# A fused attention and expert kernel: the switch from its first phase to its second is recut (22 tiles and four full pairs instead of 20 and three)

## The chip, the cores and the metric

The kernel runs on one core of one Trainium2 chip. The metric is device time in microseconds (us) of one execution; smaller is better. Engine names: PE is TensorE (matrix multiply), PEld its weight loads, DVE is VectorE, ACT is ScalarE, POOL is GpSimd, SP is SyncE; the letter q behind an engine (SPq) means instructions that only its queue handles, such as the issue of a DMA.

## What is computed

Three stages, one behind the other, all in float32. 3072 tokens (4 batches of 768) with 384 numbers each run through all of them.

```python
# 1. linear attention with a complex decay, 8 heads of 48
for t in range(S):
    new_re = ar * S_re - ai * S_im
    new_im = ar * S_im + ai * S_re
    S_re, S_im = (new_re + einsum('bhd,bhe->bhde', k[t], v[t]), new_im)
    y[t] = einsum('bhd,bhde->bhe', q[t], S_re)
# 2. a dense expert: 384 -> 768 -> 384
h = np.maximum(np.maximum(x @ w1, x @ w2), x @ w3)
x = h @ w_out
# 3. one of 8 experts for each token, 384 -> 1024 -> 384
expert_idx = np.argmax(xn @ en.T / tau, axis=1)
for e in range(8):
    h = np.maximum(x[mask] @ w1[e], 0.0)
    out[mask] = gate_w[mask, None] * (h @ w2[e])
```

## The kernel before

**Phase 1** (`phase1`, L991) does stages 1 and 2 in twelve units of 256 tokens. Every operation is first recorded with a key (`KEYS`, L1061) and then issued by a list scheduler (`issue`, L233) that takes, on the engine that is free first, the ready operation with the lowest key; so all rows of phase 1 carry the line L299, where it issues them. A unit is two tiles of 128 tokens. Its last products are `px<-wo,h`, one PSUM tile for each tile of tokens; ACT then copies it (`x1s`), writes it to the DRAM tensor `x1d` and squares it, adding up a sum of squares (`ss`, one column for each of the 24 tiles).

**The first routing** (`route_early`, L932, recorded with the key `early`) looks at the first `TE` = 20 tiles only, that is units 0 to 9. From their sums of squares and logits it forms the expert of each token (`oneh`), counts them on PE (`within`), gives the first `PE` = 3 full pairs of blocks (256 tokens of one expert each, `KE` = 6 blocks of 128) to experts, writes the experts of these pairs to a table (`tab`, in the trace `btab`), builds the one-hot rows `pos` on DVE and sorts tokens into slots on PE (`slots`); out comes `srcrow`, the token in each slot. `first_rows` (L979) then gathers block 0 (`xg_0`, an indirect DMA from `x1d` by POOL) and transposes it on PE (`pxg_0`). Both are part of phase 1, and their buffers lie in its pool `pp`.

**Phase 2** (`phase2`, L1323) runs the experts in steps. Steps 0 and 1 are the two blocks of the first pair, one at a time in plain float32; then a step is a pair (blocks 2 and 3 are step 2, and so on) with operands split into two parts (`xh`, `xl`, `w1s`, `w1l`, `w2h`, `w2l`). The expert of a step is known only on the chip: `load` reads it from the table and fetches 1.5 MB of `w1` and 1.5 MB of `w2` into two queued buffers (`queue_q_buf`), and leaves the transfer out if the expert is that of the step before. Per step: `prep` makes the weight tiles out of the queued buffer (for step 0 the copies `w1s` at L1197 on DVE), `mm1` (L1243) multiplies by `w1`, `transpose` (L1220) turns the gathered rows of the next step, `mm2` (L1259) multiplies by `w2`, and POOL scatters the result to `out`. `gather` is called two steps ahead.

**The second routing** (`late_route`, L1064) takes all 24 tiles and places what the first left over: 9 more pairs (`PL`), 8 single blocks, 5 minis of 32 tokens. `LATE` (L65) puts it behind step 1. The blocks from `KE` on can be gathered only when its `srcrow` and `dstrow` (L1142, L1145) are there. `flag` (L1409), at its end, tests among other things the sums of squares (`inrange<-ss`, L1419). A mini (`small`, L1269) loads its own weights (`w1m`, `w2m`), gathers its rows (`xgm`), and its transposes (`pxm`, L1288) stand between the halves of a step's `mm1`; `WITH` (L58) lists the steps that take one, the first being step 4.

The engines run their instructions in order. In phase 2 the order on each engine is that of the tile framework's scheduler; a pool that takes over memory of an earlier pool waits for that pool's users.

Of the kernel before, what the change touches and what calls it, by code (L numbers as in the profile page):

```python
# [27 lines left out]
E = 8  # L28
# [6 lines left out]

TE, PE, PL, SG = 20, 3, 9, E
KE, KP = 2 * PE, 2 * (PE + PL)
NBLK = KP + SG  # L40
MT, MINI = 32, 5
# [4 lines left out]
def steps(order):  # L46

    out, p, s = [(0, 1), (1, 1)], 2, KP
    for c in order:
        out.append((p, 2) if c == "p" else (s, 1))  # L50
        p, s = (p + 2, s) if c == "p" else (p, s + 1)
    assert (p, s) == (KP, NBLK - SPARE)
    return out + [(i, 1) for i in range(s, NBLK)]


STEPS = steps("ppppp" "s" "pppppp")
# [41 lines left out]
def bc(ap, axis, n):  # L98

    a = ap.unsqueeze(axis)  # L100
    shape = list(a.shape)
    shape[axis] = n
    return a.to_broadcast(shape)
# [210 lines left out]
class Prog:  # L314
# [447 lines left out]
    def moe1(self, u):  # L762
# [12 lines left out]
        for f2 in range(3):  # L775
# [5 lines left out]
            h = self.tl(pm, [128, 2, W], "h", 2, f"h{u}_{f2}")  # L781
            key, q.key = q.key, u + self.KEYS["max"]
            s.copy(h, ps[0])
# [148 lines left out]
    def route_early(self):  # L932

        q = self.q
        v, s, t = q.vector, q.scalar, q.tensor
        T, N = TE, KE
        arena = self.tl(self.pp, [128, 3, L, 3 * NR], "X", 2, "arena").rearrange("p a b c -> p (a b c)")
        used = [0]

        def new(shape, name, dt=F32):  # L940
            n = math.prod(shape)
            words = n // 2 if dt == BF16 else n
            x = arena[:, used[0]:used[0] + words]
            used[0] += words
            x = x.bitcast(dt) if dt != F32 else x
            if len(shape) == 2:
                x = x.rearrange("p (a b) -> p a b", b=shape[1])
            if len(shape) == 3:
                x = x.rearrange("p (a b c) -> p a b c", b=shape[1], c=shape[2])
            return x  # L950
        lg, mx = self.choose(new, self.ss[:, :T], self.lg[:, :T], self.oh[:, :, :T])
        self.gate(new, lg, mx, self.gates[:, :T])
        rank, cnt = self.ranks(new, self.tl(self.pg, [128, 2, E, T], "g", 2, "within0"), T)
        full, st, end, taken = self.pairs_of(new, cnt, T, PE, 256, "early")
        v.tensor_copy(self.taken, taken)

        be, x = new([PE, E], "beq"), self.bef[:, :NE]
        v.tensor_tensor(be, bc(self.blk[:, :PE], 2, E), bc(end, 1, PE), op=ALU.is_ge)
        v.tensor_reduce(x[:, 1:], be, axis=AX.X, op=ALU.add)
        v.tensor_copy(x[:, :1], x[:, 1:2])  # L960
        v.tensor_copy(self.tab[:, 0, :NE], x)
        v.tensor_tensor(self.tab[:, 1, 1:NE], x[:, 1:], x[:, :NE - 1], op=ALU.not_equal)

        ok = new([E, T], "inside")
        v.scalar_tensor_tensor(ok, bc(full, 2, T), 256.0, rank, op0=ALU.mult, op1=ALU.is_gt)
        v.scalar_tensor_tensor(rank, bc(st, 2, T), 256.0, rank, op0=ALU.mult, op1=ALU.add)
        v.scalar_tensor_tensor(rank, rank, 1.0, ok, op0=ALU.add, op1=ALU.mult)
        at, val = self.slots(new, rank, T, N)
        ps = self.tl(self.pg, [128, 5 * N], "g", 2, "slots0")
        for t0 in range(0, T, 6):  # L970
            n = min(6, T - t0)
            pos = self.tl(self.pp, [128, 6, 128], "f3", 3, f"pos{t0}", BF16)[:, :n]
            v.tensor_tensor(pos, bc(self.pos128, 1, n), bc(at[:, t0:t0 + n], 2, 128), op=ALU.is_equal)
            self.place(ps, pos, val, t0)
        tok = new([N], "tok")
        self.join(tok, self.gate_of[:, :N], ps)
        v.tensor_scalar_add(self.src[:, :N], tok, -1.0)
# [13 lines left out]
    def phase1(self):  # L991
        nc, tc = self.nc, self.tc
        with ExitStack() as ctx:
# [25 lines left out]
            self.X, self.S, self.QKr, self.xt, self.C = {}, {}, {}, {}, {}  # L1019
            K = self.KEYS  # L1020
            self.load_a(0)
# [36 lines left out]
    AHEAD = 3, 8  # L1058
    SIGNS = 4
    LAZY = False  # L1060
    KEYS = {"conv": -0.9, "moe": 0.3, "mid": -1.0, "attn": -2.0, "back": -1.0, "front": -0.9, "early": 10.5, "max": 0.3}  # L1061


    def late_route(self, pool, pg):  # L1064
# [258 lines left out]
    def phase2(self):  # L1323
        tc, nc = self.tc, self.nc
        with ExitStack() as ctx:
            regs = tc.queue_regs(depth=QD, engines=[ET.SP, ET.Activation, ET.DVE], name="wr")
            qp = ctx.enter_context(tc.tile_pool(name="wq", bufs=1, reuse_waits="tile"))
            q1 = qp.queue([128, 3072], F32, regs=regs, name="q1", contiguous=True)
            q2 = qp.queue([128, 3072], F32, regs=regs, name="q2", contiguous=True)
            pg = ctx.enter_context(tc.tile_pool(name="pg2", bufs=2, space=PSUM, reuse_waits="tile"))  # L1330
            pool = ctx.enter_context(tc.tile_pool(name="m2", bufs=1, reuse_waits="tile"))
            wq = ctx.enter_context(tc.tile_pool(name="ws", bufs=1, reuse_waits="tile"))

            late_ctx = ctx.enter_context(ExitStack())
            rp = late_ctx.enter_context(tc.tile_pool(name="rtp", bufs=1, reuse_waits="tile"))
            load, gather, prep, share, transpose, mm1, mm2, st = self.moe2(pool, wq, pg, regs, q1, q2)
            late = self.late_route(rp, pg)
            gather(*STEPS[1])
            load(0)
            first = prep(*STEPS[0])  # L1340
            for _ in range(2):
                next(first)
            last = NS - SPARE
            few = iter(())
            for k, (i, n) in enumerate(STEPS[:last]):
                if k + 2 < last:
                    gather(*STEPS[k + 2])
                p, after = iter(()), k + 1 < last
                if k == 0:

                    share(*STEPS[:2])
                    p = first
                elif after:
                    load(k + 1)
                    p = prep(*STEPS[k + 1])
                if k + 1 in WITH:

                    small = self.small(pool, mp, pg, WITH.index(k + 1))
                    next(small)
                next(p, 0)  # L1360
                mm1(i, n, 0)

                for _ in few:
                    pass
                if k in WITH:
                    few = small_now
                    next(few)
                if k + 1 in WITH:
                    small_now = small
                next(p, 0)  # L1370
                mm1(i, n, 1)
                next(few, 0)
                next(p, 0)
                if after:
                    transpose(*STEPS[k + 1])
                for b in range(n):
                    next(p, 0)
                    mm2(i, n, b)
                    next(few, 0)
                for _ in p:  # L1380
                    pass
                for _ in range(LATE.count(k)):
                    next(late)
                if k == LATE[-1]:
                    late_ctx.close()

                    self.four = self.mask
                    nc.gpsimd.memset(self.four, 0.0)
                    nc.vector.tensor_reduce(self.four[:, :MT], self.ident.rearrange("p (j r) -> p r j", r=MT), axis=AX.X,
                                            op=ALU.add)  # L1390
                    mp = ctx.enter_context(tc.tile_pool(name="mp", bufs=1, reuse_waits="tile"))
# [289 lines left out]
```

## Time and profile before

| | us |
|---|---|
| three runs | 875.11, 877.49, 877.52 |
| median | 877.49 |
| the profiled execution, own time | 878.75 |
| its span in the trace | 876.9 |

Mean granted clock of PE over the span: 0.971 of full speed.

The own time of the profiled execution is 1.85 us longer. Phase 1 fills the span up to 593 us, phase 2 the rest. In the rows further down a time is the start in us from the beginning of the span; behind it stands the busy time, then engine, line, operation, output and inputs, shapes, and the number of instructions that the row takes together; a bracket gives the idle time ahead of it and what ended it.

### The profile page before, as it was taken

What the parts mean: (1) busy time and instruction counts of PE and PEld (TensorE: products, weight loads), DVE (VectorE), ACT (ScalarE), POOL (GpSimd) and SP (SyncE); (2) the same over time, 40 slices, a digit from 0 to 9 for tenths busy, and PEclk for the clock granted to TensorE, in tenths of its full rate; (3) what the DMA queues carried; (4) which work ended last, traced back from release to release, by engine and by line L of the source; (5) the groups of instructions that cost most, each with busy time, mean ns of one, the idle gap of its engine ahead of it and who ended that gap; (6) DMA issues with size and microseconds to landing.
All of it is one profiled execution on the core that took longest, in us unless ns stands there. A gap on an engine that the chain in (4) does not pass through costs nothing. (4 is left out here: it accounts for less than half of the span.)

```text
span 876.9 us, 17518 instructions
## 1 busy us (share of the span) xinstructions
PE 813.1 (93%) x6741; PEld 714.6 (81%) x6741; DVE 643.4 (73%) x1371; ACT 434.1 (50%) x918; POOL 133.1 (15%) x195
## 2 busy tenths in 40 slices
PE   0877899999999999999999999998978999999996
PEld 0655697979797988888797979888968889789986
DVE  5998899899898989998998854357984553545531
ACT  7887636344555535564536252117434563645521
POOL 5541100010100000000001010021023323222201
PEclk9889899999999999999999999999998999999998
DMA  8642062535525171706072432051036757485200
GB/s 308 259 109 37 19 155 61 131 99 92 149 49 158 27 176 29 172 20 177 19 173 60 95 74 45 19 190 37 20 140 236 308 212 293 155 311 204 98 19 23
DMA packets 38989, 108.67 MB, mean 124 GB/s; under 512 B 5460, under 2 KB 27011, under 8 KB 35824
## 3 DMA queue, kind: packets, MB, share of 16 engines
q1 hardware_dynamic: 30032, 77.15, 30.8%
q0 software_dynamic: 8320, 29.52, 9.9%
q8 instruction: 55, 0.90, 0.4%
q10 hardware_dynamic: 544, 0.79, 0.3%
q14 instruction: 38, 0.31, 0.1%
HBM read 97.92 MB, written 10.62 MB: 124 GB/s over the span
## 5 line engine op out<-in xcount | busy, mean ns | idle before, releaser
L299 PE MATMUL ph<-xhi,whi 128*128 128x256 f32 x648 | 117.0, 289 | 0.4 <-DVE slotgate L299 0.4
L299 PE MATMUL ph<-xlo,whi 128*128 128x256 f32 x648 | 112.8, 283 | 0.0
L299 PE MATMUL ph<-xhi,wlo 128*128 128x256 f32 x648 | 112.8, 283 | 0.0
L299 PEld LDWEIGHTS ph<-xhi,whi 128*128 128x128 f32 x648 | 93.5, 192 | 2.7 <-PE slots L299 0.5
L299 PEld LDWEIGHTS ph<-xlo,whi 128*128 128x128 f32 x648 | 93.2, 192 | 0.0
L299 PEld LDWEIGHTS ph<-xhi,wlo 128*128 128x128 f32 x648 | 93.1, 191 | 0.0
L1243 PE MATMUL ph<-xh,w1s 128*128 128x256 f32 x264 | 77.0, 291 | 1.2 <-DVE hlo L1248 1.2
L1205 DVE TENSOR_TENSOR w2l<-queue_q_buf,w2h 128x768 fp32r<-128x768 f32 x52 | 47.8, 954 | 38.9 <-ACT w2h L1204 38.7
L1259 PE MATMUL py<-w2h,hhi 128*128 128x384 f32 x200 | 71.2, 356 | 5.2 <-ACT hhi L1247 5.2
L1243 PE MATMUL ph<-xh,w1l 128*128 128x256 f32 x264 | 74.6, 283 | 0.0
L1243 PE MATMUL ph<-xl,w1s 128*128 128x256 f32 x264 | 74.6, 282 | 0.0
L1259 PE MATMUL py<-w2h,hlo 128*128 128x384 f32 x200 | 70.9, 355 | 3.3 <-DVE hlo L1248 3.0
L299 PE MATMUL px<-wo,h 128*128 128x392 f32 x192 | 71.2, 502 | 0.0
L1259 PE MATMUL py<-w2l,hhi 128*128 128x384 f32 x200 | 69.6, 348 | 0.0
L1248 DVE SCALAR_TENSOR_TENSOR hlo<-ph,hhi 128x512 fp32r<-128x512 f32 x50 | 34.3, 687 | 47.4 <-ACT hhi L1247 47.4
L299 DVE TENSOR_TENSOR h<-ph,h 128x512 f32<-128x512 f32 x72 | 49.6, 689 | 25.7 <-PE ph L299 23.6
L299 PEld LDWEIGHTS pa<-S 112*128 112x128 f32 x384 | 50.1, 196 | 8.9 <-ACT kt L299 4.7
L299 PE MATMUL pa<-S 112*128 112x128 f32 x384 | 53.2, 282 | 4.2 <-ACT kt L299 4.2
L299 PE MATMUL py<-at,v 128*64 128x128 f32 (+1 forms) x576 | 56.4, 276 | 0.4 <-DVE at L299 0.4
L1243 PEld LDWEIGHTS ph<-xh,w1s 128*128 128x128 f32 x264 | 50.4, 191 | 4.6 <-issue 2.5
L1247 ACT ACTIVATE hhi<-ph 128x512 fp32r<-128x512 f32 x50 | 29.7, 597 | 48.9 <-PE ph L1243 48.7
L299 PE MATMUL py<-S,Ts 112*64 112x128 f32 x480 | 51.5, 291 | 0.0
(405 smaller groups left out, 1843.7 us busy)
## 6 DMA issues: line engine op xcount, KB each, us to landing
queue_q_buf<-w SPq DMA_DIRECT2D x26, 1536.0 KB
S<-QK SPq DMA_DIRECT2D x46, 289.1 KB
QKr<-qk SPq DMA_DIRECT2D x11, 768.0 KB
X<-a SPq DMA_DIRECT2D x10, 768.0 KB
w1m<-w SPq DMA_DIRECT2D x5, 1536.0 KB
w2m<-w SPq DMA_DIRECT2D x5, 1536.0 KB
v<-v POOLq DMA_DIRECT2D x24, 288.0 KB
x1d<-x1s SPq DMA_DIRECT2D x20, 192.0 KB
```

The costliest lines, as they stand in the source:

```text
L299: getattr(getattr(self.nc, c[0]), c[1])(*c[2], **c[3])
L1205: v.tensor_sub(lo, bv[:, c], hi.bitcast(F32))
L1243: t.matmul(ph[:, f], a, b, start=o == 0, stop=o == len(ops) - 1)
L1247: s.activation(hi, ph, AF.Relu).ins,
L1248: v.scalar_tensor_tensor(lo, ph, 0.0, hi.bitcast(F32), op0=ALU.max, op1=ALU.subtract).ins]
L1259: t.matmul(py, a[:, f, r], c[:, k % 4], start=o == 0, stop=o == 3 * KF - 1)
```

## The change

- `TE` goes from 20 to 22, `PE` from 3 to 4, `PL` from 9 to 8: the first routing waits for unit 10, too, and gives out four full pairs (8 blocks); the number of pairs, blocks and steps stays. The key `early` goes from 10.5 to 11.25.
- The five operations that write the table in `route_early` get a key lower by one than their neighbours.
- In `phase2` the pool `m2` (the gathered rows and the activations) is allocated ahead of the pool `wq` of the two queued weight buffers, so that these lie further up in memory, on addresses that the attention's tiles held, and the rows of phase 2 lie where the queued buffers were.
- `mm1` of step 1 is issued in step 0, both halves, right behind the transposes for step 1 and ahead of `mm2` of step 0; at its own place it is left out.

```diff
-TE, PE, PL, SG = 20, 3, 9, E
+TE, PE, PL, SG = 22, 4, 8, E
...
         be, x = new([PE, E], "beq"), self.bef[:, :NE]
+        key, q.key = q.key, q.key - 1.0
         v.tensor_tensor(be, bc(self.blk[:, :PE], 2, E), bc(end, 1, PE), op=ALU.is_ge)
         v.tensor_reduce(x[:, 1:], be, axis=AX.X, op=ALU.add)
         v.tensor_copy(x[:, :1], x[:, 1:2])
         v.tensor_copy(self.tab[:, 0, :NE], x)
         v.tensor_tensor(self.tab[:, 1, 1:NE], x[:, 1:], x[:, :NE - 1], op=ALU.not_equal)
+        q.key = key
...
-    KEYS = {"conv": -0.9, "moe": 0.3, "mid": -1.0, "attn": -2.0, "back": -1.0, "front": -0.9, "early": 10.5, "max": 0.3}
+    KEYS = {"conv": -0.9, "moe": 0.3, "mid": -1.0, "attn": -2.0, "back": -1.0, "front": -0.9, "early": 11.25, "max": 0.3}
...
             regs = tc.queue_regs(depth=QD, engines=[ET.SP, ET.Activation, ET.DVE], name="wr")
+
+            pool = ctx.enter_context(tc.tile_pool(name="m2", bufs=1, reuse_waits="tile"))
             qp = ctx.enter_context(tc.tile_pool(name="wq", bufs=1, reuse_waits="tile"))
...
-            pool = ctx.enter_context(tc.tile_pool(name="m2", bufs=1, reuse_waits="tile"))
...
                 next(p, 0)
-                mm1(i, n, 0)
+                if k != 1:
+                    mm1(i, n, 0)
...
                 next(p, 0)
-                mm1(i, n, 1)
+                if k != 1:
+                    mm1(i, n, 1)
...
                     transpose(*STEPS[k + 1])
+                if k == 0:
+
+                    for h in range(2):
+                        mm1(*STEPS[1], h)
```

In the changed file the lines of phase 2 have moved by two (L1243 is L1245, L1259 is L1261, L1197 is L1199, L1288 is L1290) and `inrange<-ss` by nine (L1428).

**Where PE goes over from phase 1 to phase 2.** Before, the last products of unit 11, then the first half of step 0 (`xT_99` is block 0, turned long before), then one block's transposes and `mm2` of step 0:

```order
L299 MATMUL px_11_0_1059<-wo,h_1_1070 128x392 x2
L299 MATMUL px_11_1_1060<-wo,h_1_1070 128x392 x2
L299 MATMUL px_11_0_1059<-wo,h_2_1074 128x392 x2
L299 MATMUL px_11_1_1060<-wo,h_2_1074 128x392 x2
L1243 MATMUL ph_0_0_6846<-xT_99,w1s_0_6828 128x128 x12
...
L1220 MATMUL pxg_0_6885<-ident,xg_6770 128x128 x3
L1259 MATMUL py_0_6892<-w2h_0_6830,hhi_0_0_6859 128x384
```

and after:

```order
L299 MATMUL px_11_0_1059<-wo,h_1_1070 128x392 x2
L299 MATMUL pxg_1085<-ident,xg_1084 128x128 x3
...
L299 MATMUL px_11_0_1059<-wo,h_2_1074 128x392 x2
L299 MATMUL px_11_1_1060<-wo,h_2_1074 128x392 x2
...
L1222 MATMUL pxg_0_6888<-ident,xg_6773 128x128 x3
L1222 MATMUL pxg_0_7042<-ident,xg_6839 128x128 x3
L1222 MATMUL pxg_1_7048<-ident,xg_6843 128x128 x3
L1245 MATMUL ph_0_0_6849<-xT_99,w1s_0_6831 128x128 x12
L1245 MATMUL ph_1_0_6868<-xT_99,w1s_1_6832 128x128 x12
L1245 MATMUL ph_0_0_6893<-xT_6887,w1s_0_6831 128x128 x12
...
L1261 MATMUL py_0_6929<-w2h_0_6833,hhi_0_0_6862 128x384
```

The transposes of block 0 (`pxg_1085`) have moved from 65 matmuls ahead of the end of unit 11 to 6 ahead of it; those of blocks 1, 2 and 3 stand ahead of the first product of phase 2, and the products of steps 0 and 1 by `w1` are one run.

**The same place on DVE**, before (`w1s` are the first copies of expert weights):

```order
L299 TENSOR_TENSOR h_2_1074<-ph_2_2_1073,h_2_1074 128x512
...
L1197 COPY w1s_0_6828<-queue_q_buf 128x1536
...
L1197 COPY w1s_1_6829<-queue_q_buf 128x1536
...
L1205 TENSOR_TENSOR w2l_0_6831<-queue_q_buf,w2h_0_6830 128x768
L1419 TENSOR_SCALAR inrange<-ss 128x24
```

and after:

```order
L299 TENSOR_TENSOR h_2_1074<-ph_2_2_1073,h_2_1074 128x512
...
L1428 TENSOR_SCALAR inrange<-ss 128x24
...
L1199 COPY w1s_0_6831<-queue_q_buf 128x1536
...
L1199 COPY w1s_1_6832<-queue_q_buf 128x1536
L1228 TENSOR_TENSOR xl_7041<-pxg_0_7042,xh_7040 128x3x128
```

The test of the sums of squares, which reads all 24 of them, has moved from behind the weight copies to ahead of them.

**PE behind the second routing** (`pxg` are the transposes of a pair's gathered blocks, `pxm` those of the mini). Before:

```order
L920 MATMUL slots<-ohval,ohpos_7250 128x155
L1259 MATMUL py_0_7741<-w2h_0_7359,hlo_0_1_7672 128x384
...
L1220 MATMUL pxg_0_7727<-ident,xg_7288 128x128 x3
...
L1220 MATMUL pxg_1_7733<-ident,xg_7292 128x128 x3
...
L1243 MATMUL ph_0_0_7882<-xh_7725,w1s_0_7619 128x256
```

and after:

```order
L1245 MATMUL ph_0_0_7885<-xh_7728,w1s_0_7622 128x256
L1430 MATMUL oksum<-inrange,ones 128x102
...
L1290 MATMUL pxm_7931<-ident,xgm_7602 128x32 x3
...
L1297 MATMUL phm_7985<-w1m_7598,xm_7935 32x256 x12
L1222 MATMUL pxg_0_8004<-ident,xg_7544 128x128 x3
L1222 MATMUL pxg_1_8010<-ident,xg_7548 128x128 x3
```

Before, the first gathered rows that PE needs behind the last `slots` are those of step 4 (`xg_7288`), 12 products further on; after, step 4 is among the pairs of the first routing, and the first such rows are the mini's (`xgm_7602`), 45 products further on.

## Rows read from the trace of the kernel before

**Rows 1.** The page, busy time of PE: us, share of the span, instructions.

```profile
PE 813.1 (93%) x6741; PEld 714.6 (81%) x6741; DVE 643.4 (73%) x1371; ACT 434.1 (50%) x918; POOL 133.1 (15%) x195
```

**Rows 2.** Timeline of PE, the end of phase 1 and step 0.

```profile
579.98 0.49 PE L299 MATMUL pxg<-ident,xg 128*128 128x128 f32 x3
...
587.83 5.43 PE L299 MATMUL px<-wo,h 128*128 128x392 f32 x16
593.10 5.52 PE L1243 MATMUL ph<-xT,w1s 128*128 128x128 f32 x48
...
600.06 0.44 PE L1259 MATMUL py<-w2h,hhi 128*128 128x384 f32 x1 [1.11 <-ACT hhi L1247]
...
601.95 0.69 PE L1259 MATMUL py<-w2h,hlo 128*128 128x384 f32 x1 [1.28 <-DVE hlo L1248]
```

**Rows 3.** Two stretches by window: length, busy time by engine, PEclk, DMA share, GB/s.

```profile
600.00:607.00 7.00, 5.66 (x24) 5.35 (x25) 7.00 (x8) 5.56 (x10) 0.27 (x1) 0.76 0.10 28
660.00:668.00 8.00, 7.71 (x31) 7.20 (x32) 3.72 (x5) 1.88 (x4) 3.15 (x3) 0.60 0.78 278
```

**Rows 4.** Timeline of PE, from the second routing to step 5.

```profile
617.42 0.49 PE L858 MATMUL within<-oneh,ones 128*128 128x192 f32 x2
...
648.55 0.59 PE L920 MATMUL slots<-ohval,ohpos 128*128 128x155 bf16 x6
650.91 0.45 PE L1259 MATMUL py<-w2h,hlo 128*128 128x384 f32 x1 [1.77 <-DVE hlo L1248]
...
660.11 0.90 PE L1220 MATMUL pxg<-ident,xg 128*128 128x128 f32 x3 [6.62 <-DMA xg<-x1d,srcrow]
...
667.42 0.28 PE L1243 MATMUL ph<-xh,w1s 128*128 128x256 f32 x1
...
668.72 0.28 PE L1243 MATMUL ph<-xl,w1s 128*128 128x256 f32 x1
...
676.62 1.50 PE L1295 MATMUL phm<-w1m,xm 128*32 128x256 f32 x24
...
679.12 0.34 PE L1259 MATMUL py<-w2h,hlo 128*128 128x384 f32 x1
...
681.90 0.33 PE L1259 MATMUL py<-w2h,hhi 128*128 128x384 f32 x1
```

**Rows 5.** Timeline of DVE: first routing, weight copies, end of the second routing.

```profile
564.94 0.49 DVE L299 TENSOR_TENSOR_SCAN arena<-arena,within 128x160 f32<-128x160 f32 x1 [5.12 <-PE within L299]
...
570.67 3.02 DVE L299 TENSOR_TENSOR pos<-pos,arena 128x768 bf16<-128x768 f32 x4
573.61 0.16 DVE L299 CAST btab<-bef 128x4 int32<-128x4 f32 x1
...
574.67 0.17 DVE L299 TENSOR_SCALAR srcrow<-arena 128x6 int32<-128x6 f32 x1
...
589.03 3.41 DVE L1197 COPY w1s<-queue_q_buf 128x1536 f32 x2 [0.31 <-DMA queue_q_buf<-w]
...
595.98 0.18 DVE L1419 TENSOR_SCALAR inrange<-ss 128x24 f32<-128x24 f32 x1
...
651.56 0.18 DVE L1145 CAST dstrow<-empty 128x31 int32<-128x31 f32 x1
```

**Rows 6.** Timeline of SPq: the first weight load, the first mini's weights.

```profile
581.60 0.48 SPq L1168 DMA_DIRECT2D queue_q_buf<-w  x1
...
649.26 0.35 SPq L1279 DMA_DIRECT2D w1m<-w  x1
```

**Rows 7.** Timeline of ACT: the last sum of squares of phase 1.

```profile
595.75 0.19 ACT L299 ACTIVATION_READ_ACCUMULATOR px<-px 128x1 f32 x1
```

**Rows 8.** Timeline of POOL: first gather, and the gathers behind the second routing.

```profile
575.68 1.10 POOL L299 DMA_INDIRECT xg<-x1d,srcrow  x1 [55.09 <-DVE h L299]
...
652.22 2.17 POOL L1174 DMA_INDIRECT xg<-x1d,srcrow  x1 [14.47 <-DVE dstrow L1145]
...
656.02 1.01 POOL L1174 DMA_INDIRECT xg<-x1d,srcrow  x1 [0.30 <-issue]
```

## The prediction

> **What bounds the kernel now.** The page's busy table comes first: PE is busy 93% of the span [rows 1], so only time in which PE waits, or runs at its lower clock, can be won or lost. The change touches two such places, read next in PE's timeline. At the switch from phase 1 to phase 2 [rows 2] PE goes straight from the last `px` products into step 0 at 593.10, then waits 1.11 us for ACT and 1.28 us for DVE. The windows [rows 3] give the cost behind it: from 600 to 607 the granted clock is 0.76 of full speed, so 7 × 0.24 = 1.7 us are lost to the lower of the two levels (1.2 instead of 2.4 GHz), part of it during the waits themselves. I put the switch's loss at 2.4 us of waits and 1.4 us of slow products, **3.8 us**. Behind the second routing [rows 4] PE waits 1.77 us for DVE and 6.62 us for the gathered rows of step 4; from 660 to 668 the clock is 0.60 [rows 3], 8 × 0.40 = 3.2 us. That is 1.8 + 6.6 + 3.2, **11.6 us**. Together 15.4 us: more than this the change cannot win.
>
> **First routing (TE, PE, early key).** The counting matmuls `within` stood directly ahead of unit 11's first products; the changed order has 81 of these ahead of them. A product of this shape costs 0.118 us: the 11 steps between the rows at 667.42 and 668.72 take 1.30 us [rows 4]. So the scan at 564.94 [rows 5] moves to about 574.6, **9.7 us later**. From scan to `srcrow` it is 9.73 us before [rows 5]; two tiles more of 20 add a tenth, 1 us: `srcrow` at 585.4. The last `pos` moves from 573.7 to about 583.9, and PE, which reaches its `slots` at 581.9 in the new order, waits some 1.2 us there. From `srcrow` to the transposes of block 0 it was 5.3 us at most (574.67 to 579.98, where PE was busy until then) [rows 2, 5]: at most 590.7. PE reaches them about 590.4, so that wait is 0 to 0.3 us. Phase 1's products end at 593.1 + 1.5 = **594.6**.
>
> **The table ahead of the routing's rest.** `btab` was complete 8.7 us behind the scan [rows 5]; moved ahead of the slot arithmetic it comes some 3.3 us behind it (the sum of the rows between them by their order), at 577.9. That is still 4 us later than before, since the scan is later. It serves the load of step 0 alone, and only if nothing else holds that load.
>
> **The weight buffers on the attention's memory.** The first load was issued at 581.60 [rows 6], 1.1 us behind the transposes of block 0 (579.98 + 0.5) [rows 2], though the table was ready at 573.6 [rows 5]. In the changed order the load still lists waits on the gather of block 0, its PE transposes and the routing's arithmetic: all of them belong to the pool that the buffers take over. I therefore take the load to stay behind those transposes, now at 590.9: issue at 592.0, 10.4 us later than before. This is my choice, and a rival below drops it. From the end of those transposes to the first `w1s` copy it was 589.03 − 580.5 = 8.5 us [rows 5]: copy at 599.4. One of the two copies is half of 3.41 us: step 0's first product at **601.2**.
>
> **inrange ahead of the copies.** DVE now must pass `inrange`, which needs the last sum of squares: 595.75 before [rows 7], 2.7 us behind the end of phase 1's products, so 597.3 now, and DVE goes on at 597.7. Behind it are queued the two `w1s` copies, and PE waits for them. With the load as late as above this costs nothing (597.7 is before 599.4); with an early load it is what holds the copies.
>
> **First blocks interleaved.** PE has nine transposes to do behind 594.6 (0.49 us for three [rows 2]), until some 595.7. Then it has nothing until 601.2: the products of step 1 cannot fill the gap, because they read the same `w1s`. Idle 5.5 us. The slow stretch behind it is bounded by the two rows at hand: 1.4 us behind waits of 2.4 us, 3.2 us behind 6.6 us; I take 2.8. In return the waits of 1.11 and 1.28 us go, since 48 products lie between a conversion and its use. Step 0's `w2` lands with the load 10 us later; it has 96 products of 0.11 us (5.52 us for 48 [rows 2]) as cover, which is about enough. The switch's loss is then 8.3 us: **+4.5** against 3.8, and with the 1.5 us of phase 1 the second routing's `within` moves from 617.42 [rows 4] to 623.4, **+6.0**.
>
> **Step 4 out of the second routing.** From that `within` to the last slots PE has 146 products of 0.118 us, 12 block transposes of 0.16, 96 `py` of 0.174 (16 steps between 679.12 and 681.90 [rows 4]) and 24 slot products of about 0.1 (0.59 for six): 38 us. The last slots end at S = 661.5. `dstrow` took 2.8 us behind them and the first gather went out 3.3 us behind them [rows 4, 5, 8]. Now PE does not need step 4's rows: it has 45 products, 5.3 us, until the mini's transposes `pxm`. POOL gives out the two gathers of step 5 first and the mini's third, as the third one at 656.02 [rows 8], S + 7.1. Its flight is bounded by two rows: 4.3 us alone (575.68 to 579.98 at most), 7.9 us beside the weight loads (652.22 to 660.11) [rows 2, 4, 8]. The mini's `w1m` still goes out right at the slots [rows 6], so some crowding is sure: landing at S + 11.4 to S + 15, taken in the middle, S + 13. PE waits 13 − 5.3 = 7.7 us (6.1 to 9.7) and then runs slow for 2.8 us: 10.5 us where it lost 11.6, **−1.1** (−2.7 to +0.9).
>
> The Trainium skill, "DMA: Bandwidth & Descriptors", section "SWDGE vs HWDGE vs iDMA", speaks against a gather being crowded out: it says that the two kinds of DMA feed different internal queues of an engine, and that the engine goes round-robin between them. The trace's 7.9 us against 4.3 us shows that sharing alone nearly doubles a flight; by the rule alone the uncrowded end holds, and the sum below would be 1.6 us lower.
>
> **The sum.** +6.0 − 1.1 = **+4.9 us**. On the profiled execution's 878.75 us this is 883.65; the median of the runs is 1.26 us lower, so the forecast is **882.4 us**. All behind step 4 is untouched: same steps, same loads.
>
> **Rivals.**
> - *The late gap closes.* The second routing has 38 us of PE's work between `within` and the last slots, against 31 before (617.42 to 648.94); if PE is held up there by nothing and the gathers fly alone and go out at once, the mini's rows land close to S + 5.3, where PE wants them. Then the 11.6 us go: 6.0 − 11.6 = −5.6, **872 us**; with a switch that loses 3 us less, 869. For it: the pair moved out is the one PE waited 6.62 us for. Against: in the new order `slots` stand behind 42 of step 3's 48 `py`, so S is no earlier relative to `pxm`.
> - *The load does go early.* If the buffers' new place frees the load, it is issued at 579 and landed at 586.5, but `inrange` holds the copies to 597.7: first product at 599.5, 1.7 us earlier than forecast. Together with the uncrowded gather: +4.9 − 1.7 − 1.6, **879 us**, no difference that can be measured. That the load lies on other addresses than block 0's rows speaks for it; the waits that the order lists speak against it.
> - *The mini queues behind all weights.* The late stall is then not one gather but `w1m`, `w2m` and a load, 4.7 MB at the 278 GB/s of the second window [rows 3], 17 us from S + 0.3: PE waits 11.7 us and runs slow for 3.2, +3.3 against 11.6; with the switch's +6.0, **886.8 us**. It decides from a landing at S + 14 on, where the late place loses more than before. For it: the weights' DMAs are issued before the gather is. Against: the crowded flight of 7.9 us ended beside such loads, too.
>
> **How the numbers follow.** A measurement of this kernel tells 0.3%, 2.6 us, from no change: faster is below 874.9, slower above 880.1. Forecast 0.42, mini behind all weights 0.13, together slower 0.55. Late gap closed: 0.20, faster. Early load, or smaller ends of the terms: 0.25, same. The range reaches from 869 (gap closed and quick switch) to 888 (last rival and a bad slots wait). The likeliest case's own range is 880.5 to 884.5, by the bounds of the mini's landing.
>
> **What would show it.** Right: the first weight load issued near 592, behind block 0's transposes; PE idle 5 us ahead of `ph<-xT,w1s`, released by `w1s`; `inrange` ahead of the copies on DVE; `within` near 623; no wait at step 4's `pxg`, but one of 6 to 9 us at `pxm`, released by `xgm`. Wrong: a load issued near 579; a first product before 598; `pxm` without a wait, or with one above 11 us.

## The result, and the profile after

The changed kernel takes 886.0 us (median of 7 runs, 878.25 to 888.13) against 876.42 us before (median of 7); the ratio is 1.0094, with a 95% interval from 1.0071 to 1.0116. It is slower by a little under 1%, as forecast, and inside the range. By medians it is 9.6 us, by the ratio 8.2, where 4.9 were forecast. One execution before, of 1973.21 us, is left out of the ratio.

Its profiled execution is one of its shorter ones: 881.7 us, span 879.9. I read it first at the switch. On PE (start, busy time, instruction, and in the bracket the wait ahead of it and its releaser), to be held against [rows 2]:

```profile
590.20 0.49 PE L299 MATMUL pxg<-ident,xg 128*128 128x128 f32 x3
590.53 4.12 PE L299 MATMUL px<-wo,h 128*128 128x392 f32 x12
594.48 0.82 PE L1222 MATMUL pxg<-ident,xg 128*128 128x128 f32 x6
599.30 0.59 PE L1222 MATMUL pxg<-ident,xg 128*128 128x128 f32 x3 [4.00 <-ACT xT L1224]
601.77 13.23 PE L1245 MATMUL ph<-xT,w1s 128*128 128x128 f32 x96 [1.88 <-DVE w1s L1199]
...
623.18 0.49 PE L858 MATMUL within<-oneh,ones 128*128 128x192 f32 x2
```

Phase 1's products end near 594.6, and PE does next to nothing until 601.77: two waits of 4.00 and 1.88 us stand where 1.11 and 1.28 stood. `within`, which ends this place, comes 5.8 us later than in [rows 4]. What PE waited for is on SP's queue and on DVE (compare [rows 5, 6]):

```profile
590.89 1.09 SPq L1170 DMA_DIRECT2D queue_q_buf<-w  x1
...
661.84 0.35 SPq L1281 DMA_DIRECT2D w1m<-w  x1
663.10 0.34 SPq L1282 DMA_DIRECT2D w2m<-w  x1
...
668.35 0.69 SPq L1171 DMA_DIRECT2D queue_q_buf<-w  x1
```

```profile
574.61 0.52 DVE L299 TENSOR_TENSOR_SCAN arena<-arena,within 128x176 f32<-128x176 f32 x1 [0.56 <-PE within L299]
...
577.66 0.17 DVE L299 CAST btab<-bef 128x5 int32<-128x5 f32 x1
...
585.22 0.17 DVE L299 TENSOR_SCALAR srcrow<-arena 128x8 int32<-128x8 f32 x1
...
598.91 0.18 DVE L1428 TENSOR_SCALAR inrange<-ss 128x24 f32<-128x24 f32 x1 [9.13 <-ACT px L299]
599.96 3.41 DVE L1199 COPY w1s<-queue_q_buf 128x1536 f32 x2 [0.87 <-PE pxg L1222]
```

The table is there at 577.8, the first load goes out at 590.89, right behind block 0's transposes, and the copies follow 9 us behind it. The other place is behind the second routing (PE, then POOL):

```profile
661.14 0.57 PE L920 MATMUL slots<-ohval,ohpos 128*128 128x145 bf16 x6
...
678.03 0.52 PE L1290 MATMUL pxm<-ident,xgm 32*128 32x32 f32 x3 [10.62 <-DMA xgm<-x1d,srcrow]
683.02 1.50 PE L1297 MATMUL phm<-w1m,xm 128*32 128x256 f32 x24
```

```profile
664.56 1.05 POOL L1176 DMA_INDIRECT xg<-x1d,srcrow  x1 [0.30 <-PE ph L1245]
665.91 1.03 POOL L1176 DMA_INDIRECT xg<-x1d,srcrow  x1 [0.30 <-issue]
667.25 1.01 POOL L1284 DMA_INDIRECT xgm<-x1d,srcrow  x1 [0.31 <-PE ph L1245]
```

The waits of 1.77 and 6.62 us [rows 4] are gone, and one of 10.62 us for the mini's rows has come. The windows (length, then busy time and instructions of PE, PEld, DVE, ACT and POOL, then PEclk, DMA share, GB/s) show what is behind both waits:

```profile
602.00:604.00 2.00, 2.00 (x10) 2.00 (x11) 2.00 (x3) 0.00 (x0) 0.00 (x0) 0.50 0.61 204
604.00:606.00 2.00, 2.00 (x12) 2.00 (x11) 1.74 (x12) 0.50 (x2) 0.20 (x1) 0.50 0.39 149
606.00:608.00 2.00, 2.00 (x17) 2.00 (x17) 0.47 (x2) 1.00 (x2) 0.00 (x0) 0.87 0.00 0
...
668.00:676.00 8.00, 0.00 (x0) 0.00 (x0) 0.25 (x1) 0.00 (x0) 1.27 (x2) 0.71 1.02 393
676.00:680.00 4.00, 1.97 (x10) 1.91 (x11) 0.00 (x0) 0.24 (x1) 1.01 (x1) 0.50 0.99 397
680.00:684.00 4.00, 4.00 (x40) 3.52 (x43) 0.94 (x2) 1.20 (x2) 0.00 (x0) 0.80 0.52 220
```

Behind the first wait 1 + 1 + 0.3 = 2.3 us are lost to the lower clock level. While PE waits for the mini's rows the DMA engines are busy all the time, at 393 to 397 GB/s; behind this wait 1.0 + 0.8 = 1.8 us of busy time are lost to the lower level (half of the 1.97 us busy from 676 to 680, and a fifth of the next four). The mini's products start 6.4 us later than in [rows 4] (683.02 against 676.62). At the span's end 3.0 of them are left in this pair of profiles, because the execution before ran at the lower clock for a while behind two 2 us waits near 703 and 782 (0.83 of full clock from 700 to 710 and from 780 to 790, 3.4 us together), and this one did not. Medians, not this pair, give the size.

### The profile page after: what moved, and what is told of

Read it like the earlier page. It is cut to its first block, busy times and chain, and to the rows that moved or that the text cites. A ratio compares the mean times of both kernels' runs of the same rounds, so it can differ in the third digit from the quotient of the medians.

```text
span 879.9 us, 17510 instructions
## 1 busy us (share of the span) xinstructions
PE 808.4 (92%) x6747; PEld 711.3 (81%) x6747; DVE 646.7 (73%) x1371; ACT 435.3 (49%) x918; POOL 132.9 (15%) x194
## 3 DMA queue, kind: packets, MB, share of 16 engines
HBM read 97.92 MB, written 10.62 MB: 123 GB/s over the span
## 5 line engine op out<-in xcount | busy, mean ns | idle before, releaser
L1245 PE MATMUL ph<-xh,w1s 128*128 128x256 f32 x264 | 77.6, 294 | 1.2 <-DVE hlo L1250 1.2
L1245 PE MATMUL ph<-xl,w1s 128*128 128x256 f32 x264 | 75.1, 286 | 0.0
L1245 PE MATMUL ph<-xh,w1l 128*128 128x256 f32 x264 | 75.1, 285 | 0.0
L1261 PE MATMUL py<-w2h,hhi 128*128 128x384 f32 x200 | 68.8, 344 | 2.7 <-ACT hhi L1249 2.7
L1261 PE MATMUL py<-w2h,hlo 128*128 128x384 f32 x200 | 67.5, 338 | 1.3 <-DVE hlo L1250 1.1
L1261 PE MATMUL py<-w2l,hhi 128*128 128x384 f32 x200 | 66.9, 335 | 0.0
L299 ACT COPY h<-ph 128x512 f32<-128x512 f32 x36 | 21.1, 587 | 72.5 <-PE ph L299 62.5
L1245 PEld LDWEIGHTS ph<-xh,w1s 128*128 128x128 f32 x264 | 51.1, 194 | 4.6 <-issue 2.5
```

What stands on the lines that cost most here:

```text
L299: getattr(getattr(self.nc, c[0]), c[1])(*c[2], **c[3])
L1245: t.matmul(ph[:, f], a, b, start=o == 0, stop=o == len(ops) - 1)
L1261: t.matmul(py, a[:, f, r], c[:, k % 4], start=o == 0, stop=o == 3 * KF - 1)
```

## The experiments

A point that serves all of them: the executions start phase 2 at different times. The last `px<-wo,h` run of unit 10, of 16 matmuls, starts at 558.92 before and at 558.83 after, but between 557.17 and 562.68 in the other profiles, most of it in code that is the same. Times below with a plus are counted from that row; before, the first product of step 0 comes at +34.18, `within` at +58.50 and the mini's products at +117.70. What lies behind it repeats to a few hundredths until the gathers and loads come in. Ratios are to the kernel before, run beside.

**e1_again**: the changed kernel, nothing edited.

> The changed kernel once more, for a second profile of it, since its seven times fall into 878 to 882 and 886 to 888 us and its one profile is of the lower group. Theory of the two waits: both waits (5.9 us at the switch, 10.6 us at the mini's transposes) are there in every execution, and the groups differ behind them, in whether PE runs slow after the short waits near 709, 752 and 785 us. Rival: the groups differ in the two waits themselves (a load or a gather that lands 5 us later). Times again in both groups, median 882 to 887 us.

884.08 us, 1.0100 (1.0073 to 1.0128), all six times within 1.4 us. Its waits are those of the first profile: 3.87 and 1.57 us at the switch, `within` at +64.82 (+64.35), 11.15 us at `pxm`, the mini's products at +126.04 (+124.19). No second group showed, so the question of two groups stays open; the two waits are in both executions.

**e2_inrange_late**: the test of the sums of squares behind the copies.

```diff
+        self.big = new([1], "big")
+        v.tensor_scalar(self.big, cnt[:, :1], 0.0, 1e38, op0=ALU.mult, op1=ALU.add)
...
-        v.tensor_scalar(ok[:, n - NTILE:], self.ss, 1e38, None, op0=ALU.is_lt)
+        v.tensor_tensor(ok[:, n - NTILE:], self.ss, bc(self.big, 1, NTILE), op=ALU.is_lt)
```

> The test of the sums of squares is tied to a value of the second routing, so that DVE reaches it behind the weight copies. Theory of the load: the copies start when the weights have landed, near 599.5 as now (599.96), and the time moves by under 1 us. Rival, inrange: the copies were held by the test (ended 599.09), they start 3 us or more earlier and the time falls by 3 to 5 us.

884.83 us, 1.0098 (1.0069 to 1.0128): no change. The copies start at +40.16 (+41.13 and +42.47 in the two profiles of the changed kernel), `within` at +64.03, the mini's products at +126.09. So `inrange` held the copies by 1 to 2 us and the end by nothing that shows; it was not what bound the switch.

**e3_own_buffer**: block 0's rows outside the pool that the weight buffers take over.

```diff
-        xg = self.tl(self.pp, [128, DM], "f3", 3, "xg_0")
+        xg = self.tl(self.pm, [128, DM], "xg0", 1, "xg_0")
```

> The rows of block 0 get a buffer outside the pool that the weight buffers take over, so that the first load waits for the slots (584.5) and srcrow (585.2) instead of block 0's transposes (590.5). Theory of the load: issue near 585.7 instead of 590.9, copies 8.5 us behind at 594.2, first product of step 0 near 596 instead of 601.8, the slow stretch behind it gone; 6 to 8 us off everything up to the second routing, so 876 to 880 us with the late wait still 9 to 11 us. Rival, the load is bound by its transfer or by the third block's transposes (599.3): the first product stays behind 599 and the gain is at most 2 us.

881.51 us, 1.0062 (1.0037 to 1.0087). The load goes out at 588.70, that is +26.84 against +32.06, 5.2 us earlier, and the copies start at +34.59 against +41.13: the load's wait was that of block 0's rows, and the copies follow the load. But the first product came at +40.34, only 2.6 us earlier than the +42.94 of the changed kernel. PE and POOL (in that order) of this run tell why:

```profile
596.17 0.55 PE L299 MATMUL pxg<-ident,xg 128*128 128x128 f32 x3 [2.77 <-DMA xg<-x1d,srcrow]
```

```profile
588.73 1.10 POOL L299 DMA_INDIRECT xg<-x1d,srcrow  x1 [68.68 <-DVE slotgate L299]
```

Load and gather of block 0 now leave together (588.70 and 588.73); from `srcrow` to the transposes it takes 7.9 us instead of 5.0, and PE waits 2.77 us in the middle of unit 11's last products. Behind the wait it runs at 0.75, 0.50 and 0.89 of full clock from 596 to 602 (windows of 2 us, 1.7 us lost), and these products end at +40.5 instead of +35.8. Most of what the early load won is given back there. The edit also moved more than the load, since the order in phase 2 is the scheduler's:

```profile
602.20 5.52 PE L1245 MATMUL ph<-xT,w1s 128*128 128x128 f32 x48
607.56 0.49 PE L1222 MATMUL pxg<-ident,xg 128*128 128x128 f32 x3
```

The nine transposes ahead of the first product and the one run of steps 0 and 1 are gone, waits of 0.51 and 0.89 us for step 0's conversions are back, and `inrange` stands behind the copies. So e3 shows what held the load, not what an early load alone is worth. The mini's products come at +121.51, earlier than in both profiles of the changed kernel (+124.19, +126.04). The time lies lower than the changed kernel's, but the intervals overlap.

**e4_mini_gather_first**: POOL gathers the mini's rows ahead of step 5's.

```diff
-                if k + 2 < last:
+                if k + 2 < last and k + 1 not in WITH:
                     gather(*STEPS[k + 2])
...
                     next(small)
+                    if k + 2 < last:
+                        gather(*STEPS[k + 2])
```

> POOL gathers the mini's rows ahead of those of step 5 instead of behind them: the gather is issued 2.7 us earlier (664.6 instead of 667.3). Theory, gathers land in the order of their issue and late because of the weight loads: the rows land 2 to 4 us earlier, the wait of 10.6 us at the mini's transposes falls to 7 to 8.5, the time by 2 to 4 us. Rival, all the DMAs share and the end is set by the three loads' 4.7 MB: the wait stays over 10 us, the time does not change.

```profile
678.82 0.52 PE L1290 MATMUL pxm<-ident,xgm 32*128 32x32 f32 x3 [7.90 <-DMA xgm<-x1d,srcrow]
```

884.09 us, 1.0090 (1.0058 to 1.0123). The wait falls from 10.62 to 7.90 us, as the first theory had it, with 9.7 us in flight (669.09 to 678.82) instead of 10.8, and the mini's products come at +122.61 instead of +124.19 or +126.04. The total does not show it: 884.09 us here, 884.08 in e1_again.

**e5_pairs_only**: four pairs from the 20 tiles of before.

```diff
-TE, PE, PL, SG = 20, 3, 9, E
+TE, PE, PL, SG = 20, 4, 8, E
```

> The kernel before with four full pairs from its 20 tiles (PE 4, PL 8, TE 20, key 10.5): the first routing stays where it was. Theory, the switch's loss comes with the 22 tiles and the late wait with the pairs: the switch is that of before (first product 34.2 us behind the start of unit 10's last px), the rows of step 4 are there in time, and PE waits for the mini's rows instead, 5 to 9 us; the time is that of before or up to 3 us less. Rival, four pairs alone cost what the change cost: 883 us or more.

```profile
668.40 0.53 PE L1288 MATMUL pxm<-ident,xgm 32*128 32x32 f32 x3 [7.29 <-DMA xgm<-x1d,srcrow]
```

877.38 us, 1.0010 (0.9984 to 1.0036): no difference. The switch is that of before (waits of 1.11 and 1.28 us), and the wait at step 4's transposes has turned into one of 7.29 us for the mini. Its products come at +114.77, 2.9 us earlier than before, and the time does not show that either.

That 20 tiles hold four full pairs is true of the inputs of this case, and not of all inputs. Of their 2560 tokens up to 8 × 255 = 2040 can lie outside full pairs, so only 520 are sure to lie inside, and these need three pairs (two hold 512); with 22 tiles, 2816 tokens, 776 are sure, and these need four (three hold 768). e5, e8, e11 and e12 leave this assurance out: by the code of `route_early` the table's entry for a missing pair would count to 8, and the experts are 0 to 7.

**e6_all_but_tiles**: the table's keys, the pools' order and the interleaved blocks, with the numbers of before.

```diff
-TE, PE, PL, SG = 22, 4, 8, E
+TE, PE, PL, SG = 20, 3, 9, E
...
-"early": 11.25
+"early": 10.5
```

> The changed kernel with the numbers of before (TE 20, PE 3, PL 9, key 10.5), that is, the table's keys, the pools' order and the interleaved first blocks alone. Theory: none of the three moves the end, the time is that of before within 2 us, and the first load still goes out behind block 0's transposes. Rival, the buffers' new place or the interleaving are what costs: 878 us or more.

877.88 us, 1.0025 (1.0002 to 1.0047): at most half a percent. In its profile PE waits 1.35 and 1.28 us at the switch and 6.69 us at step 4's transposes, as before. The first load goes out at 579.89 where block 0's transposes start at 578.27: still behind them.

**e9_tiles_only**: 22 tiles and their key, three pairs.

```diff
-TE, PE, PL, SG = 20, 3, 9, E
+TE, PE, PL, SG = 22, 3, 9, E
...
-"early": 10.5
+"early": 11.25
```

> The kernel before with the first routing over 22 tiles and its key of 11.25, but three pairs as before (PE 3, PL 9). Theory, the 22 tiles alone bring the late switch: the first product of step 0 starts 42 to 44.5 us behind the start of unit 10's last px instead of 34.2, and the late wait at step 4's transposes stays, 6 to 9 us: 880 to 886 us. Rival, the loss needs the four pairs too: within 3 us of before.

```profile
598.85 0.90 PE L1220 MATMUL pxg<-ident,xg 128*128 128x128 f32 x3 [3.88 <-ACT xT L1222]
600.99 7.61 PE L1243 MATMUL ph<-xT,w1s 128*128 128x128 f32 x48 [1.24 <-DVE w1s L1197]
...
668.99 1.54 PE L1220 MATMUL pxg<-ident,xg 128*128 128x128 f32 x6 [5.79 <-DMA xg<-x1d,srcrow]
```

885.96 us, 1.0113 (1.0087 to 1.0140): the whole loss of the change, with the changed kernel's waits at the switch (first product at +42.05) and a late wait of 3.35 us for `dstrow` and 5.79 us for step 4's rows. `within` comes at +63.80, 5.3 us later than before, and the mini's products at +124.65, 7.0 us later: most of the loss arises at the switch. Tiles and key were not parted: the key of 11.25 goes with unit 10, and no run has one without the other.

**e7_minis_later**: the changed kernel with the first mini in step 5.

```diff
-WITH = 4, 6, 8, 10, 12
+WITH = 5, 7, 9, 11, 12
```

> The changed kernel with the first mini one step later (WITH 5, 7, 9, 11, 12): behind the second routing the first rows that PE needs are those of step 5, and the mini's two weight loads no longer go out at the slots. Theory, the late wait is the mini's gather crowded by weight loads: no wait above 3 us behind the second routing, and 8 to 12 us less: 873 to 877 us. Rival, the first gather behind the second routing is late whatever it is for: a wait of 5 us or more at step 5's transposes, and at most 4 us less.

```profile
674.51 0.55 PE L1222 MATMUL pxg<-ident,xg 128*128 128x128 f32 x3 [3.55 <-DMA xg<-x1d,srcrow]
676.82 0.90 PE L1222 MATMUL pxg<-ident,xg 128*128 128x128 f32 x3 [1.76 <-DMA xg<-x1d,srcrow]
```

877.97 us, 1.0030 (1.0004 to 1.0055), some 6 us below the changed kernel. Two waits of 3.55 and 1.76 us for step 5's rows remain, between the two theories' bounds. One thing in the expectation was wrong: the mini's weights still go out right behind the slots (662.29); it is only that PE needs the rows later.

**e10_minis_only**, the same edit of `WITH` in the kernel before; **e8_pairs_minis_later** and **e11_best_again**, that edit with the one of e5.

> The kernel before with the first mini one step later (WITH 5, 7, 9, 11, 12) and nothing else. Theory: step 4's gathered rows are still the first that PE needs behind the second routing, the wait at its transposes stays over 5 us and the time within 3 us of before; the gain of the version with four pairs needs both. Rival, the minis' weights are what crowds that gather: the wait falls below 4 us and the time by 4 us or more.

> The kernel before with four pairs from 20 tiles and the minis one step later: neither the late switch nor the mini's rows right behind the second routing. Theory: both losses of the changed kernel are gone and the late one of before (11.6 us) too; 6 to 10 us below before, 865 to 869 us. Rival, another wait takes the late place (the weights of the mini at the next step, or the gather of step 5): within 3 us of before.

> The version with four pairs from 20 tiles and the minis one step later once more, beside the next one on the same chip. Both theories: 5 to 9 us below before.

e10: 875.29 us, 0.9992 (0.9968 to 1.0016), with a wait of 6.61 us at step 4's transposes. e8: 869.46 us, 0.9912 (0.9878 to 0.9946); e11: 868.58 us, 0.9915 (0.9895 to 0.9935). Either edit alone gives nothing, both together 0.85%. What is left behind the second routing in e8:

```profile
657.96 0.44 PE L1259 MATMUL py<-w2h,hlo 128*128 128x384 f32 x1 [1.53 <-DVE hlo L1248]
...
686.23 0.50 PE L1288 MATMUL pxm<-ident,xgm 32*128 32x32 f32 x3 [2.60 <-DMA xgm<-x1d,srcrow]
```

**e12_best_late_earlier**: e11 with the second routing called behind step 0.

```diff
-LATE = 1, 1
+LATE = 0, 0
```

> The same with the second routing called behind step 0 instead of step 1 (LATE 0, 0). Theory, what is left of the late place (1.5 us for DVE, 2.6 us for the mini's rows) goes when the slots come earlier: 2 to 5 us below the version without it. Rival, DVE is full there (19.8 of 20 us between 640 and 660 in the changed kernel), so that earlier routing makes a step's weights late: no gain, or a new wait of PE for w1l or w2l of 2 us or more.

```profile
646.54 0.57 PE L920 MATMUL slots<-ohval,ohpos 128*128 128x145 bf16 x6 [0.30 <-DVE ohpos L1137]
648.99 0.55 PE L1243 MATMUL ph<-xh,w1s 128*128 128x256 f32 x1 [1.89 <-DVE tok L927]
```

870.93 us, 0.9944 (0.9920 to 0.9969): not better than e11. No wait for gathered rows is left, but PE waits 3.35 us in five pieces at the slots for DVE, the last two shown. So the rival holds in its first half, no gain; that DVE has no room there fits these waits, but was not tested apart.

## Why the prediction was right, and where it was not

- **First routing, 9.7 us later; srcrow at 585.4; phase 1's end at 594.6.** Measured: scan at 574.61, `srcrow` at 585.22, table at 577.66, phase 1's end near 594.6. Right, to 0.2 us.
- **The load stays behind block 0's transposes.** Issue at 590.89 (592.0 predicted), copies at 599.96 (599.4), first product at 601.77 (601.2). Right, and borne out by e3, where another buffer for block 0's rows let the load out 5.2 us earlier. The rival of the early load fell.
- **inrange.** Passed at 598.91 (597.3 predicted), a little ahead of the copies; e2 shows that it costs nothing at the end.
- **PE idle 5.5 us, 2.8 us of slow products.** 5.88 and 2.3: the sum is right because two small errors cancel, and I had PE idle in one piece behind all nine transposes. In fact the third block's transposes wait 4.00 us for ACT, which copies `xT` at 598.78 behind its last sums of squares. By these rows they would have held the first product to some 599.9 (599.30 + 0.59) even with an early load; no run shows that, since in e3 they stand elsewhere.
- **The interleaving takes the waits of 1.11 and 1.28 us away.** In the changed kernel they are gone. But the edit is not what took them away: with 20 tiles, in e6, it leaves 1.35 and 1.28, and in e9, 22 tiles without the edit, no wait of PE there is longer than 0.26. In e9 the 48 products ahead of them ran slow (7.61 us, 5.52 before); in e3, 22 tiles too, these ran in 5.52 us and waits of 0.51 and 0.89 are back. That fits slow products that give the conversions time, but no run tests it.
- **`within` at 623.4, last slots at 661.5.** 623.18 and 661.7 (661.14 + 0.57). Right. (The end of the last slots before, 648.94 in the prediction, is 649.14 by its row, 648.55 + 0.59; the distances taken from it, 2.8, 3.3 and 7.1 us, are 0.2 us too long.)
- **The mini's rows, the term that was mis-sized: "landing at S + 11.4 to S + 15, taken in the middle, S + 13", a late place of −1.1 us.** The gather went out earlier than predicted (667.25, S + 5.5 instead of S + 7.1), but was 10.8 us in flight (11.05 in e1_again), more than the 7.9 us that I had as its upper bound: rows at S + 16.3. PE waited 10.62 us instead of 7.7, above the 6 to 9 us named as the sign of being right; the 11.15 us of e1_again are above the 11 us named as the sign of being wrong. With 1.8 us of slow products behind the wait it is 12.4 against 11.6, **+0.8** instead of −1.1. The rows agree: from `within` to the mini's products it takes 59.84 us against 59.20 before, +0.6, and 61.22 in e1_again, +2.0.

The bound of 7.9 us came from a gather that was the first in POOL's queue and ran beside three weight transfers: the mini's two and the next step's `w1`. The `w2` behind them went out only after the rows had landed (660.11), as SP's queue in the kernel before shows:

```profile
655.51 0.35 SPq L1168 DMA_DIRECT2D queue_q_buf<-w  x1
666.57 0.35 SPq L1169 DMA_DIRECT2D queue_q_buf<-w  x1
```

In the changed kernel the mini's gather is the third of its queue and all four transfers are under way beside it; in e1_again the last two go out at 668.46 and 669.15. By the windows the DMA engines move 7.5 MB from 662 to 684 against 5.9 MB from 650 to 666 before, which is four and three transfers of 1.57 MB and six indirect ones of 0.2 MB. The place in the queue counts, as e4 shows (wait 7.90 us, flight 9.7); that the fourth transfer makes up the rest is argued and not tested. e7 bears the late place out: with PE's need pushed back, 5.3 us in two pieces are left of the wait.

The last rival (a wait of 11.7 us, 886.8 us, chance 0.13) comes near with its wait. By the median, 886.0, its time is nearer than the forecast's 882.4; by the ratio, 884.7, the two are equally far. Its mechanism, a landing behind all the weights, is not what e4 shows: there the rows land at 678.82, and the DMA engines go on at over 400 GB/s until 686.

The Trainium skill, "DMA: Bandwidth & Descriptors", section "SWDGE vs HWDGE vs iDMA", has the two kinds of DMA served in turn from different queues. The 10.8 us of this gather, while the DMA engines moved 393 to 397 GB/s, show that being served in turn does not keep a gather of one block short; that it does get a share agrees with e4, where the rows landed 7 us ahead of the end of the same four loads.

- **The parts.** By the runs: tiles and key 1.0113, pairs 1.0010, all the rest 1.0025, the change 1.0094. The late switch accounts for the loss. e7 and e8 say the same, run beside the same executions of the kernel before: both have four pairs and the later minis, e7 has the 22 tiles, their key and the other three edits besides, and it takes 877.97 us against 869.46. The fourth pair by itself only gives the late wait another name. Why the medians differ by 8 to 10 us, when the mini's products come 6.5 to 8.3 us later, is open in its last 2 us; the clock in later stretches differs from execution to execution by more.

## What to carry to other kernels

Taking work off one late wait is worth only what the next thing in the same queue allows: here the fourth pair gained nothing until the mini, next in line behind the same routing, was moved too, and then both together gave 0.85%. Giving an early stage more input (22 tiles for 20) delays all that hangs on its end, so weigh what the larger input is needed for: with the inputs of this case four pairs could be had from 20 tiles, and the 22 pay for having them with any input. A buffer on other addresses need not free a load: with the new place alone (e6) it went out behind block 0's transposes as before, and it went early when the rows were taken out of the earlier pool (e3), which fits a wait for the pool as a whole. And an early load that leaves together with a gather that PE needs is paid for by the gather.

## What the runs showed of the hardware that was not expected

The same wait can be followed by products at the lower clock level, or not. In e8 and e11, one program, PE waits 1.11 and 1.28 us at the switch, to the hundredth, and has done the same before (first product at +34.40 and +34.39). By the windows of 600 to 605 and 605 to 610 (length, PE, PEclk, DMA share, GB/s) of e8

```profile
600.00:605.00 5.00, 2.61 (x20) 0.92 0.17 46
605.00:610.00 5.00, 5.00 (x17) 0.50 0.00 0
```

and of e11

```profile
600.00:605.00 5.00, 3.72 (x22) 1.00 0.14 39
605.00:610.00 5.00, 5.00 (x44) 1.00 0.10 39
```

the second half runs at 1.2 GHz in the one and at 2.4 in the other, and `within` comes at +60.18 and +57.37: the same 2.4 us of waiting cost 2.8 us more in one execution than in the other. The two ran on different chips, but that is not what decides: e5, on the chip of e8 and with the same two waits, runs at full clock behind them (1.00 from 605 to 610, `within` at +57.40). I had priced such a stretch at a fixed 1.4 to 3.2 us; it is a matter of the execution, and one profile of each kernel does not tell a difference of 3 us.
